# The first load of y as eight transfers of 16 partitions in place of one of 128

## The chip, the cores and the metric

The kernel runs on one core of one Trainium2 chip. The metric is the device time of one execution in microseconds (us), lower being better. The median of three runs of the kernel before is 119.94 us (119.94 to 120.14).

## The reference

```python
B, S, D = 1024, 16, 512
x, y:  bfloat16 (B, S, D)        gamma: bfloat16 (D)

def reference(x, y, gamma):
    return x + gamma * y
```

Every row of 512 numbers of y is multiplied by the same gamma and added to the row of x. Read and written are x, y and the output, of 16.78 MB each: 50.33 MB in all.

## The kernel before

The 16,384 rows of x, y and the output are dealt out to the 128 partitions of SBUF: partition p holds rows 128 p to 128 p + 127, which lie one after the other in DRAM (L52 to L54). "Rows" from here on are the 128 rows of one partition, of 1,024 bytes each. The whole of y stays in SBUF (`y_sb`, 128 rows in each partition) and is worked on in place: it is multiplied by gamma, then x is added into it, then it is stored. x has a buffer of 64 rows only (`x_sb`), which is loaded twice.

The work is written down as lists, without a scheduler:

- `SP` (L10) is what the SyncE queue issues, in this order: y rows 0 to 64, x rows 0 to 64, y rows 64 to 128, x rows 64 to 117, x rows 117 to 128. The last two go into places of `x_sb` that earlier rows held, so SP waits for the adds that free them (`frees`, L85; the wait is at L107).
- `ACT` (L11) is what the ScalarE queue issues: the row of gamma, then the stores of rows 0 to 64 and 64 to 128. The first store waits also until x rows 64 to 117 have landed (`RELEASE`, L16; TensorE passes the news on at L135 to L137).
- `DVE` (L18) is the order on VectorE: multiplies ('m') and adds ('a') of four pieces of 53, 11, 53 and 11 rows (`PIECES`, L6): m0, m1, a0, a1, m2, m3, a2, a3. Each is one instruction over 128 partitions (L156, L165). `need` (L141) puts the waits for the loads ahead of them: m0 waits for the y load that holds its rows, a0 for the x load.

The function `ring` (L96) walks through such a list and issues one DMA for each entry. One load of 64 rows is a DMA of 128 partitions, each with 64 rows that lie one after the other in DRAM and in SBUF, 65,536 bytes. Every load has a semaphore of its own, which a finished DMA raises by 16; `_take` (L22) waits for a count and takes it off again. VectorE waits for 16 before the first use of a load (L147).

`EARLY` (L13) says how many entries of each list are issued before everything else. The last lines (L173 to L179) take these DMA instructions out of their place and put them at the head of the program, ahead of the barrier at which the engines meet at its beginning (it appears in the waits as L41). It is (1, 0): the first load of y is issued there, before SP goes to the barrier; the other loads and gamma are issued after it.

gamma is spread over the partitions with a matmul of a row of ones with the row of gamma (L130), which VectorE copies to SBUF as bfloat16 (L132). The first multiply needs it.

Of the kernel before, what the change touches and what calls it, by code (L numbers as in the profile page):

```python
# [15 lines left out]
RELEASE = ('x', 64, 117, 0)  # L16

DVE = [('m', 0), ('m', 1), ('a', 0), ('a', 1), ('m', 2), ('m', 3), ('a', 2), ('a', 3)]  # L18
MULT, ADD = mybir.AluOpType.mult, mybir.AluOpType.add


def _take(sem, n, eng):  # L22


    return eng.wait_ge(sem, n).then_inc(sem, -n)  # L25


def kernel(
# [9 lines left out]
    nc = tc.nc  # L38
    P = nc.NUM_PARTITIONS
# [13 lines left out]
    yv = yf.rearrange("(p n) d -> p n d", p=P)  # L53
# [5 lines left out]
    y_sb = nc.alloc_sbuf_tensor("y_sb", [P, rows, D], dt).ap()  # L59
    x_loads = [w for w in SP + ACT if w[0] == "x"]  # L60
    y_loads = [w for w in SP + ACT if w[0] == "y"]
# [9 lines left out]
    s_load = {w: sem("s_" + "_".join(map(str, w[:2]))) for w in x_loads + y_loads}  # L71
    s_add, s_go, s_rel, s_end, s_out = sem("s_add"), sem("s_go"), sem("s_rel"), sem("s_end"), sem("s_out")
    added = [a for kind, *a in DVE if kind == "a"]
    order = {a[0]: k for k, a in enumerate(added)}

    def meets(a, b, c, d):
        return a < d and c < b

    def pieces_of(a, b):
        return [c for c in range(n) if meets(starts[c], starts[c + 1], a, b)]  # L80
# [4 lines left out]
    def frees(w):  # L85

        c = set()
        for v in x_loads[: x_loads.index(w)]:
            lo, hi = max(v[3], w[3]), min(v[3] + v[2] - v[1], w[3] + w[2] - w[1])
            if lo < hi:  # L90
                c |= set(pieces_of(v[1] + lo - v[3], v[1] + hi - v[3]))
        return sorted(c)

    early = []

    def ring(eng, what, n_early):  # L96

        known, went = 0, False
        for k, w in enumerate(what):
            kind = w[0]  # L100
            need = frees(w) if kind == "x" else pieces_of(w[1], w[2]) + list(w[3:]) if kind == "s" else []
            need = max((order[c] + 1 for c in need), default=0)
            if kind == "s" and not went:
                _take(s_go, 1, eng)
                went = True
            if need > known:
                eng.wait_ge(s_add, need)  # L107
                known = need
            if kind == "g":
                i = eng.dma_start(out=gamma_row, in_=gamma.unsqueeze(0)).then_inc(s_gamma, 16)  # L110
            elif kind == "x":
                to = x_sb[:, w[3] : w[3] + w[2] - w[1], :]
                i = eng.dma_start(out=to, in_=xv[:, w[1] : w[2], :]).then_inc(s_load[w], 16)
            elif kind == "y":
                r = slice(w[1], w[2])
                i = eng.dma_start(out=y_sb[:, r, :], in_=yv[:, r, :]).then_inc(s_load[w], 16)
            else:
                r = slice(w[1], w[2])
                i = eng.dma_start(out=ov[:, r, :], in_=y_sb[:, r, :]).then_inc(s_out, 16)
            if k < n_early:  # L120
                early.append(i.ins)

    ring(nc.sync, SP, EARLY[0])
    ring(nc.scalar, ACT, EARLY[1])


# [14 lines left out]
    def need(loads, c):  # L141
        for w in loads:
            if w not in landed and meets(starts[c], starts[c + 1], w[1], w[2]):
                if w == RELEASE:
                    _take(s_rel, 1, nc.vector)
                else:
                    _take(s_load[w], 16, nc.vector)  # L147
                landed.add(w)

    for kind, *args in DVE:  # L150
        c = args[0]
        yt = y_sb[:, starts[c] : starts[c + 1], :]
        if kind == "m":
            need(y_loads, c)
            g = gamma_sb[:, None, :].to_broadcast([P, PIECES[c], D])
            nc.vector.tensor_tensor(out=yt, in0=yt, in1=g, op=MULT).then_inc(s_dve, 1)  # L156
            open_mults += 1
        else:
            need(x_loads, c)
            if open_mults:  # L160
                _take(s_dve, open_mults, nc.vector)
                open_mults = 0
            at = x_at(starts[c])
            xt = x_sb[:, at : at + PIECES[c], :]
            nc.vector.tensor_tensor(out=yt, in0=xt, in1=yt, op=ADD).then_inc(s_add, 1)  # L165
# [44 lines left out]
```

## Time and profile before

| what | before |
|---|---|
| median of 3 runs | 119.94 us |
| the profiled execution | 119.93 us |
| its span, first to last instruction | 118.6 us |
| multiply or add of 53 rows (L156, L165) | 14.3 us each, two of either |
| multiply or add of 11 rows | 3.1 us each, two of either |
| first multiply starts | 21.94 us |
| first add starts | 41.39 us |
| reloads of x issued on SP | from 55.71 us |
| stores issued on ACT | from 76.88 us |
| HBM read and written | 33.56 and 16.78 MB |

The span starts with the first instruction, which is SP's issue of the first load of y. An engine's busy time counts its instructions; a DMA instruction only issues, and its packets then run on the core's 16 DMA engines, of which the page shows the busy share and the bytes moved in slices of time. A packet is counted in the slice in which it starts, with its whole length, so that shares above 1 occur in short slices. Queue q1 is SP's, q10 is ACT's. The small packets of a few bytes are those that raise the semaphores.

### The profile page before, as it was taken

Reading aid. Unit: us, or ns where it says so; the run is one execution under the profiler, and the core shown is the slowest. Engines: PE = TensorE matmul, PEld = TensorE weight load, DVE = VectorE, ACT = ScalarE, POOL = GpSimd, SP = SyncE. Lnnn points to the kernel's source line nnn. Section 1 sums busy time; section 2 is a strip of 40 time slices with the busy share of each in tenths; the row PEclk is TensorE's granted clock in tenths of the full one; section 3 lists DMA queues with packets and bytes.
Section 4 is the critical chain, followed back from the end, with each engine's and each line's share of the span. In section 5 each row is a group of like instructions: output and inputs, shape, how many; then the busy total and the mean of one; then the engine's idle time right before and its main releaser. Section 6 shows DMA issues by size and latency. Waiting matters only on the chain. (4 is left out here: it accounts for less than half of the span.)

```text
span 118.6 us, 78 instructions
## 1 busy us (share of the span) xinstructions
PE 0.6 (0%) x1; PEld 0.1 (0%) x1; DVE 70.0 (59%) x10; POOL 0.2 (0%) x4
## 2 busy tenths in 40 slices
PE   0001000000000000000000000000000000000000
PEld 0000000000000000000000000000000000000000
DVE  0002000599999299999759999999999910000000
POOL 0000000000000000000000000000000000000000
DMA  9889888998899888998896969598899888988892
GB/s 354 354 376 685 354 354 354 597 464 354 354 398 663 354 354 354 663 398 354 354 586 293 586 293 567 220 639 354 354 575 486 354 354 376 685 354 354 354 619 88
DMA packets 1010, 50.33 MB, mean 424 GB/s; under 512 B 113, under 2 KB 114, under 8 KB 114
## 3 DMA queue, kind: packets, MB, share of 16 engines
q1 hardware_dynamic: 720, 33.55, 66.0%
q10 hardware_dynamic: 290, 16.78, 32.6%
HBM read 33.56 MB, written 16.78 MB: 424 GB/s over the span
## 5 line engine op out<-in xcount | busy, mean ns | idle before, releaser
L156 DVE TENSOR_TENSOR y_sb<-y_sb,gamma_sb 128x27136 bf16<-128x27136 bf16 (+1 forms) x4 | 34.6, 8688 | 12.7 <-DVEq L25 12.7
L165 DVE TENSOR_TENSOR y_sb<-x_sb,y_sb 128x27136 bf16<-128x27136 bf16 (+1 forms) x4 | 34.6, 8688 | 2.3 <-DVEq L25 2.2
L132 DVE CAST gamma_sb<-gamma_ps 128x512 bf16<-128x512 f32 x1 | 0.7, 692 | 8.8 <-DVEq L25 8.8
L127 DVE MEMSET ones_row<- 1x128 bf16 x1 | 0.2, 165 | 1.5 <-PEq L41 1.5
L130 PE MATMUL gamma_ps<-gamma_row,ones_row 1*128 1x512 bf16 x1 | 0.6, 578 | 9.7 <-PEq L25 9.7
L130 PEld LDWEIGHTS gamma_ps<-gamma_row,ones_row 1*128 1x128 bf16 x1 | 0.1, 100 | 9.7 <-issue 9.7
L194 POOL MEMSET const-uint8-127<- 128x1 uint8 x1 | 0.1, 102 | 0.0
L194 POOL MEMSET const-bfloat16-1.0<- 128x1 bf16 x1 | 0.1, 101 | 0.0
L194 POOL MEMSET const-float32-0.0<- 128x1 f32 x1 | 0.1, 98 | 0.2 <-issue 0.2
L194 POOL MEMSET const-float32-1.0<- 128x1 f32 x1 | 0.1, 98 | 0.0
## 6 DMA issues: line engine op xcount, KB each, us to landing
x_sb<-in_x_dram SPq DMA_DIRECT2D x1, 6784.0 KB, 20.8
x_sb<-in_x_dram SPq DMA_DIRECT2D x1, 1408.0 KB, 23.9
y_sb<-in_y_dram SPq DMA_DIRECT2D x2, 40.2
out_dram<-y_sb ACTq DMA_DIRECT2D x2, 22.8
x_sb<-in_x_dram SPq DMA_DIRECT2D x1, 39.7
gamma_row<-in_gamma_dram ACTq DMA_DIRECT2D x1, 1.0 KB
```

What stands on the lines that cost most here:

```text
L127: nc.vector.memset(ones_row, 1.0).then_inc(s_ones, 1)
L130: nc.tensor.matmul(gamma_ps, ones_row, gamma_row, start=True, stop=True).then_inc(s_ps, 1)
L132: nc.vector.tensor_copy(out=gamma_sb, in_=gamma_ps).then_inc(s_dve, 1)
L156: nc.vector.tensor_tensor(out=yt, in0=yt, in1=g, op=MULT).then_inc(s_dve, 1)
L165: nc.vector.tensor_tensor(out=yt, in0=xt, in1=yt, op=ADD).then_inc(s_add, 1)
L194: nc = _bacc.Bacc("TRN2", target_bir_lowering=False, num_devices=1)
```

## The change

The first entry of the list with y, rows 0 to 64, is issued as eight DMAs. DMA number j takes the partitions j, j + 8, j + 16 and so on to j + 120, 16 in all, with the same 65,536 bytes for each partition; together they move the same bytes to the same places. All eight are put at the head of the program, ahead of the barrier. They raise one semaphore, and VectorE waits for 16 x 8 = 128 before the first multiply. The other loads, the stores and the arithmetic stay.

```diff
+GROUP = 8
...
             elif kind == "y":
                 r = slice(w[1], w[2])
-                i = eng.dma_start(out=y_sb[:, r, :], in_=yv[:, r, :]).then_inc(s_load[w], 16)
+
+                step = GROUP if w == y_loads[0] else 1
+                for j in range(step):
+                    to, of_ = y_sb[j:P:step, r, :], yv[j:P:step, r, :]
+                    i = eng.dma_start(out=to, in_=of_).then_inc(s_load[w], 16)
+                    if step > 1:
+                        early.append(i.ins)
...
-            if k < n_early:
+            if k < n_early and i.ins not in early and w != y_loads[0]:
                 early.append(i.ins)
...
-                    _take(s_load[w], 16, nc.vector)
+                    _take(s_load[w], 16 * GROUP if w == y_loads[0] else 16, nc.vector)
```

## The prediction

> **What bounds the kernel now.** I read the table of busy time first, then the line of the DMA engines in the 40 slices, the queues, and then short windows of the span, since the table names no bound by itself.
>
> ```profile
> span 118.6 us, 78 instructions
> PE 0.6 (0%) x1; PEld 0.1 (0%) x1; DVE 70.0 (59%) x10; POOL 0.2 (0%) x4
> ...
> DMA  9889888998899888998896969598899888988892
> ...
> DMA packets 1010, 50.33 MB, mean 424 GB/s; under 512 B 113, under 2 KB 114, under 8 KB 114
> ...
> q1 hardware_dynamic: 720, 33.55, 66.0%
> q10 hardware_dynamic: 290, 16.78, 32.6%
> ```
>
> VectorE is busy for 59% of the span, but the packets of the two queues fill 66.0 + 32.6 = 98.6% of 16 engines' time. There is no slice in which they rest. The kernel is bound by its 16 DMA engines from the first packet to the last, so a cost to the packets goes straight to the end. The chain of waits does not show this (it holds two adds and "issue"), since no instruction stands for the transfer that ends last.
>
> The length of one packet comes from windows of 1 us (columns: busy time and count of each engine, clock, share of the 16 DMA engines, GB/s; a packet is booked whole in the window in which it starts):
>
> ```profile
> 1.00:2.00 1.00, 0.00 (x0) 0.00 (x0) 0.17 (x1) 0.00 (x0) 1.00 2.92 983
> 11.00:12.00 1.00, 0.00 (x0) 0.00 (x0) 0.15 (x1) 0.00 (x0) 1.00 2.42 1049
> ```
>
> In 11 to 12 us, 1049 GB/s over 1 us is 1.049 MB, that is 16 packets of 65,536 bytes, one for each engine; a share of 2.42 says that each took 2.42 us. So an engine moves 65,536 / 2.42 = 27.1 GB/s, 16 of them 433. The 50.33 MB are 48 such packets for each engine: 48 x 2.42 = 116.2 us. What remains of the 118.6 us lies at the two ends. In 1 to 2 us, 983 GB/s is 15 packets, with a share of 2.92: 2.92 x 16 / 15 = 3.11 us each, 0.7 us more than later ones. The same view with 0.1 us windows shows when these packets start, and when the last round does:
>
> ```profile
> 0.90:1.00 0.10, 0.00 (x0) 0.00 (x0) 0.00 (x0) 0.00 (x0) 1.00 1.90 655
> 1.00:1.10 0.10, 0.00 (x0) 0.00 (x0) 0.00 (x0) 0.00 (x0) 1.00 10.09 3277
> ...
> 1.60:1.70 0.10, 0.00 (x0) 0.00 (x0) 0.08 (x1) 0.00 (x0) 1.00 1.69 655
> ```
>
> ```profile
> 4.00:4.10 0.10, 0.00 (x0) 0.00 (x0) 0.00 (x0) 0.00 (x0) 1.00 1.51 655
> ...
> 4.50:4.60 0.10, 0.00 (x0) 0.00 (x0) 0.00 (x0) 0.00 (x0) 1.00 4.54 1966
> ...
> 115.20:115.30 0.10, 0.00 (x0) 0.00 (x0) 0.00 (x0) 0.00 (x0) 1.00 1.51 655
> ...
> 115.80:115.90 0.10, 0.00 (x0) 0.00 (x0) 0.00 (x0) 0.00 (x0) 1.00 1.51 655
> ```
>
> 655 GB/s in 0.1 us is one packet. The first packets start between 0.9 and 1.7 us, the second ones between 4.0 and 4.6, the last whole ones between 115.2 and 115.9: the engine that is late at 4.6 us is late by as much at the end. Start (1.0 to 1.6) + 0.7 + 116.2 gives 117.9 to 118.5, and the last semaphore and wait end the span.
>
> [...] of packets under 512 B there are 113, which is 16 for each of seven transfers of 128 partitions and 1 for gamma's single row. [...]
>
> **The change, part by part.**
> Spreading. Transfer j touches partitions j, j+8, ..., j+120. [...] eight packets per engine. [...] a packet takes 2 x 2.42 = 4.84 us: 8 x 4.84 = 38.7 us in place of 8 x 2.42 = 19.4. That adds 19.4 us. [...] I take 19.4[...].
>
> Does anything hide it? No: the DMA engines have no slack (98.6%), and the rest follows them. The first multiply starts at 21.94 us, after 10.8 us of idle time that the landing of y ends; the first add at 41.39 us waits for x, behind y on the same rings. VectorE, the reloads of x and the stores all move back together; the idle 2.2 us before that add stay. After y the old spreading is back, at the old rate.
>
> Issuing. The trace's DMA instructions on SP take 0.37, 0.33 and 0.45 us. Eight for one are 7 x 0.37 = 2.6 us more before SP reaches the starting barrier. All engines wait there, so gamma and the first x load, issued at 1.43 us, go out near 4.0; the second y load, at 1.81, near 4.4. Cover: x must be in the rings by about 21 us, 17 us later. Gamma's chain ends with the cast at 10.46 + 0.69 = 11.15 us and would end near 13.8, 8 us ahead of the old 21.94 (and far ahead of a later one). The eight follow each other at about 0.4 us, each with 2.42 us of work, so no engine runs dry. Cost 0; only an issue of over 2.4 us would uncover it.
>
> Semaphores. 7 x 16 more small packets, 7 on each engine. At the old end of y (window 20 to 22 us: share 1.21, as in any stretch that catches one start of every engine) no gap shows. Between 0 and 0.1 us in all; I take 0.05. The wait counts to 128 in place of 16 on the same instruction, which holds up nothing else.
>
> Start. A short transfer may give all 16 engines their first descriptor sooner. If the first starts, spread over 0.6 us, fell together with the earliest, the late engines would win about 0.5 us; if the spread comes from serving 16 engines one after another, 0. I take 0.15.
>
> Sum: 19.4 + 0 + 0.05 - 0.15 = 19.3. The profiled execution took 119.93 us for a span of 118.6; the median of the runs is 119.94, so the sum is put on that: 139.2 us. The likeliest case's own range is 129.6 to 142.
>
> **Rivals.**
> A. [...] (119.6 us, the other side). [...] packets stay at 2.42 us and only the start counts: a gain of up to 0.5 us less 0.05, I take 0.3, so 119.64. [...]
> B. The same without the gain (119.9): the spread of the starts comes from the engines being served in turn. For it: a DMA instruction costs 0.52 us even for gamma's one row, so the rows do not set its length.
> C. [...] (121.4). [...] the other eight would start with the fifth issue, 4 x 0.37 = 1.5 us late (at most 4 x 0.45 = 1.8). Every engine still has 48 packets, so the end moves by the 1.5 us: 121.4. [...]
>
> **How the numbers follow.** Ports 0.66, C 0.08, B 0.11, A 0.15. No change means within 0.2%, 0.24 us, about what a measurement of this kernel can tell. A is faster, B the same; ports and C slower: 0.15, 0.11, 0.74. The range leaves out A and the tail above 142 and takes in the others: 119.7 to 142.
>
> **What would show it.** Right: from 1 to 40 us the DMA engines busy at about 217 GB/s, packets of 4.84 us; the first multiply near 41 us; from then on 2.42 us packets and every later event 19 us back; under 512 B 225 packets. If the first multiply starts before 22.2 us and packets take 2.42 us, [...] (A or B: the starts tell which). Half of the first packets starting 1.5 us late would be C. [...]

## The result, and the profile after

| | before | changed |
|---|---|---|
| median of 4 runs each | 120.0 us | 141.51 us (141.44 to 141.59) |
| profiled execution, and its span | 119.93, 118.6 us | 141.47, 140.1 us |
| first multiply starts | 21.94 us | 43.63 us |

The ratio is 1.179 (95% interval 1.177 to 1.181): the change costs 21.5 us, where the forecast had 19.3. The page of the changed kernel, its first line, the DMA engines in 40 slices, the packets and the queues:

```profile
span 140.1 us, 85 instructions
...
DMA  9929909939949697998969699798969696989976
GB/s 299 243 56 299 300 0 299 299 75 224 299 150 449 299 580 318 486 412 374 524 299 599 299 496 480 325 434 376 582 299 599 299 599 299 524 374 449 449 337 262
DMA packets 1123, 50.33 MB, mean 359 GB/s; under 512 B 226, under 2 KB 227, under 8 KB 227
...
q1 hardware_dynamic: 832, 33.56, 70.8%
q10 hardware_dynamic: 290, 16.78, 27.6%
```

The engines are still busy for 70.8 + 27.6 = 98.4% of the time, and the bytes are the same, but the mean rate fell from 424 to 359 GB/s. So the engines do not wait for work; a part of the packets takes longer. Q1's small packets rose by 112, that is by 16 for each of the seven additional transfers (one more packet of a few bytes is another queue's, q14). The twos and zeros of the DMA line are no rest: a packet is booked where it starts, and long packets leave slices without a start.

Which packets, is seen in windows of about one round each, in which 16 packets start, one for each engine (233 GB/s over 4.5 us are 1.049 MB; columns as in the prediction: window and its length, busy time and count of PE, PEld, DVE and POOL, clock, DMA share, GB/s):

```profile
1.30:5.80 4.50, 0.00 (x0) 0.00 (x0) 0.00 (x0) 0.00 (x0) 1.00 1.05 233
...
16.10:21.20 5.10, 0.58 (x1) 0.10 (x1) 0.69 (x1) 0.00 (x0) 1.00 1.00 206
21.20:26.10 4.90, 0.00 (x0) 0.00 (x0) 0.00 (x0) 0.00 (x0) 1.00 1.01 214
...
31.20:36.30 5.10, 0.00 (x0) 0.00 (x0) 0.00 (x0) 0.00 (x0) 1.00 1.01 206
...
41.40:44.60 3.20, 0.00 (x0) 0.00 (x0) 0.97 (x1) 0.00 (x0) 1.00 0.91 328
44.60:47.00 2.40, 0.00 (x0) 0.00 (x0) 2.40 (x1) 0.00 (x0) 1.00 1.01 437
```

Window length times share is the mean length of a packet: 4.7 us in the first round, 5.1 in the others, 4.9 in the fifth, then 2.9 in the round that follows y and 2.4 again from 44.6 us on. The records of the packets themselves say 4.72, 5.11, 4.94, 2.89 and 2.42. The slow packets are exactly the 128 of the first y load, eight rounds of 16. The fifth round is a little shorter than the others, and so it is in the kernels e3, e9 and e10 below (4.96, 4.93 and 4.85 us); why is not shown.

The start of the timeline (start and length in us, engine, line, operation, count, and idle time before):

```profile
0.00 5.01 SPq L122 DMA_DIRECT2D y_sb<-in_y_dram  x8
...
6.31 0.34 SPq L115 DMA_DIRECT2D x_sb<-in_x_dram  x1
6.32 0.53 ACTq L112 DMA_DIRECT2D gamma_row<-in_gamma_dram  x1
...
17.88 0.58 PE L138 MATMUL gamma_ps<-gamma_row,ones_row 1*128 1x512 bf16 x1 [17.88 <-PEq L27]
18.61 0.69 DVE L140 CAST gamma_sb<-gamma_ps 128x512 bf16<-128x512 f32 x1 [12.04 <-DVEq L27]
43.63 17.30 DVE L164 TENSOR_TENSOR y_sb<-y_sb,gamma_sb 128x27136 bf16<-128x27136 bf16 x2 [24.33 <-DVEq L27]
62.97 17.29 DVE L173 TENSOR_TENSOR y_sb<-x_sb,y_sb 128x27136 bf16<-128x27136 bf16 x2 [2.04 <-DVEq L27]
...
98.46 18.85 ACTq L127 DMA_DIRECT2D out_dram<-y_sb  x2
```

SP issues for 5.01 us ahead of the barrier, in place of 0.37; x and gamma go out 4.9 us later, and gamma is ready at 19.3 us. The multiply, at 43.63, waits 24.33 us for y alone. The rest of the kernel follows at its old distances: the first add and the stores are both 21.58 us later than before (41.39 and 76.88 us then).

### The profile page after: what moved, and what is told of

Same layout as the page of the kernel before. It is cut to its first block, busy times and chain, and to the rows that moved or that the text cites. A ratio compares the mean times of both kernels' runs of the same rounds, so it can differ in the third digit from the quotient of the medians.

```text
span 140.1 us, 85 instructions
## 1 busy us (share of the span) xinstructions
PE 0.6 (0%) x1; PEld 0.1 (0%) x1; DVE 70.0 (50%) x10; POOL 0.2 (0%) x4
## 3 DMA queue, kind: packets, MB, share of 16 engines
q1 hardware_dynamic: 832, 33.56, 70.8%
q10 hardware_dynamic: 290, 16.78, 27.6%
```

## The experiments

The suspect is the SBUF side: which partitions the engines write at the same time. "Port theory" in the expectations is the name for this assumption, that some sets of partitions make the engines hold each other up and others do not; the prediction's "ports" is the case with doubled packets. No record shows where on the way into SBUF this would happen; the runs show which sets of partitions are fast and which are slow. Its rivals: the eight issues and their semaphores; the place in DRAM, since the rows of one transfer now lie at a distance of 1 MB (8 partitions of 131,072 bytes); that each transfer has only one packet for each engine (the one-descriptor theory); the start of the program. All the edits are in the loop that issues the y load; e7 alone moves it to another load. The times of e1 and e11 are medians of 12 and 8 executions, the others are of one execution each; the kernel before took 119.87 to 120.46 us beside them, so that a difference of several us can be read from one.

**e1_row_split: eight transfers, all 128 partitions in each.**

```diff
-                    to, of_ = y_sb[j:P:step, r, :], yv[j:P:step, r, :]
+                    q = slice(w[1] + 8 * j, w[1] + 8 * j + 8)
+                    to, of_ = y_sb[:, q, :], yv[:, q, :]
```

> The first load of y is again issued as eight transfers ahead of the barrier, but each takes 8 of the 64 rows of all 128 partitions (8,192 bytes for a partition, eight descriptors for an engine). Port theory [...]: [...] the 21.5 us are gone and the time is within 0.5 us of 120.0; the first multiply starts near 22.3 us. Issue theory (eight issues, eight semaphores and a later barrier cost the time): it stays near 141. If only the start counts, the 0.4 us by which the first packet came later (1.37 in place of 1.00 us) would show how much of it is due to eight issues.

Measured: 120.2 us, ratio to before 1.0016 (1.0007 to 1.0025). From its timeline, and a window within the first y load:

```profile
0.00 4.06 SPq L123 DMA_DIRECT2D y_sb<-in_y_dram  x8
...
22.19 17.29 DVE L166 TENSOR_TENSOR y_sb<-y_sb,gamma_sb 128x27136 bf16<-128x27136 bf16 x2 [11.37 <-DVEq L27]
```

```profile
10.00:14.00 4.00, 0.00 (x0) 0.00 (x0) 0.69 (x1) 0.00 (x0) 1.00 1.01 428
```

The eight issues take 4.06 us on SP, gamma and x go out at 5.1, the first multiply starts at 22.19 us, and the rate within the load is close to the old one (428 against 433 GB/s). So eight issues ahead of the barrier with 112 more semaphore packets cost 0.2 us at most. The smaller packets alone can account for it: 309 ns for 8,192 bytes, where an eighth of 2.42 us is 302, so that the packets of this load sum to 20.37 us for each engine in place of 20.04. The issue theory falls.

**e2_next_16 and e4_sbuf_next_dram_8th, e3_sbuf_8th_dram_next: the SBUF side against the DRAM side.**

```diff
-                    to, of_ = y_sb[j:P:step, r, :], yv[j:P:step, r, :]
# e2
+                    to, of_ = y_sb[16 * j : 16 * j + 16, r, :], yv[16 * j : 16 * j + 16, r, :]
# e3
+                    to, of_ = y_sb[j:P:8, r, :], yv[16 * j : 16 * j + 16, r, :]
# e4
+                    to, of_ = y_sb[16 * j : 16 * j + 16, r, :], yv[j:P:8, r, :]
```

> Eight transfers of 16 partitions that lie next to each other (16 j to 16 j + 15) in place of every eighth. Port theory: [...] a packet takes 4 x 2.42 = 9.7 us or, with the surcharge of the changed kernel (5.11 in place of 4.84), 10.2; the load takes 77 to 82 us, the kernel 178 to 183 us. HBM theory (engines that read at a distance of 1 MB in DRAM collide): the distance is now 128 KB, the packets are back near 2.42 us and the time near 120. One-descriptor theory (a packet that is alone in its transfer, with a semaphore write after it, is slow whatever its place): 5.1 us a packet and 141.5 us as in the changed kernel.

> SBUF side as in the changed kernel (partitions j, j + 8, ...), DRAM side as with neighbours (blocks 16 j to 16 j + 15), so that the first 64 rows of y go to other partitions than their own and that half of the output is computed from other rows of y. Port theory: 5.1 us a packet, 141.5 us, since only the SBUF side counts. HBM theory: near 120. One-descriptor theory: 141.5.

> The crossed case: SBUF partitions 16 j to 16 j + 15, DRAM blocks j, j + 8, ..., so that the first 64 rows of y go to other partitions than their own and that half of the output is computed from other rows of y. Port theory: [...] 178 to 183 us, whatever the DRAM side does. HBM theory: as the changed kernel, 141.5. One-descriptor theory: 141.5.

Measured: 174.6 us (e2), 141.32 (e3), 175.64 (e4). Windows of about one round, first of e2, then of e3, then of e4:

```profile
17.90:27.10 9.20, 0.58 (x1) 0.10 (x1) 0.69 (x1) 0.00 (x0) 1.00 1.01 114
27.10:36.40 9.30, 0.00 (x0) 0.00 (x0) 0.00 (x0) 0.00 (x0) 1.00 1.00 113
```

```profile
31.30:36.40 5.10, 0.00 (x0) 0.00 (x0) 0.00 (x0) 0.00 (x0) 1.00 1.01 206
```

```profile
27.60:37.00 9.40, 0.00 (x0) 0.00 (x0) 0.00 (x0) 0.00 (x0) 1.00 1.00 112
```

The packet follows the SBUF side: 5.1 us with every eighth partition, 9.3 or 9.4 with 16 neighbours, whichever blocks of DRAM they are read from. Between e2 and e4, which differ in the DRAM side alone, lie 0.13 us a packet (9.27 and 9.40), between e3 and the changed kernel nothing (5.11 in both). The HBM theory falls, and so does the one-descriptor theory, since all four kernels have one packet for each engine in a transfer, and two of them take nearly twice as long for it as the other two. The 9.27 us are less than the 9.7 to 10.2 that were expected: the direction of the assumption is right, its arithmetic, with four times 2.42 us, only near. That factor of four was the author's estimate. By the packet records the engines start one round over 1.86 us in e2 and over 1.63 us in e4, so for that time packets of two transfers are in flight; whether this makes the packets shorter no run tests.

**e10_every_4th_of_64: which 16 partitions.**

```diff
-                    to, of_ = y_sb[j:P:step, r, :], yv[j:P:step, r, :]
+                    a = 64 * (j // 4) + j % 4
+                    to, of_ = y_sb[a : a + 61 : 4, r, :], yv[a : a + 61 : 4, r, :]
```

> Eight transfers of 16 partitions, every fourth of 64 (a, a + 4, ..., a + 60). [...] Port theory: 5.1 us a packet and about 141.4 us again. [...] as it does with 128 partitions, and the packets would be 2.42 us, about 120.4.

Measured: 140.84 us, 5.08 us a packet; the expectation's other figures, 2.42 us and 120.4, are out. One round of it:

```profile
30.70:35.80 5.10, 0.00 (x0) 0.00 (x0) 0.00 (x0) 0.00 (x0) 1.00 1.00 206
```

Every fourth of 64 partitions does as badly as every eighth of 128 (5.08 and 5.11 us), so it is not the step of eight that makes a packet slow.

**e7_second_load: not the start.** The first y load is one transfer again, and the same eight are made of the second, in their place in the list (the diff is against the kernel before):

```diff
-                i = eng.dma_start(out=y_sb[:, r, :], in_=yv[:, r, :]).then_inc(s_load[w], 16)
+                if w == y_loads[1]:
+                    for j in range(GROUP):
+                        to, of_ = y_sb[j:P:8, r, :], yv[j:P:8, r, :]
+                        i = eng.dma_start(out=to, in_=of_).then_inc(s_load[w], 16)
+                else:
+                    i = eng.dma_start(out=y_sb[:, r, :], in_=yv[:, r, :]).then_inc(s_load[w], 16)
...
-                    _take(s_load[w], 16, nc.vector)
+                    _take(s_load[w], 16 * GROUP if w == y_loads[1] else 16, nc.vector)
```

> The first load of y is one transfer again; instead the second (rows 64 to 128), which is issued at 1.8 us and runs from 40 us on, is issued as eight transfers of every eighth partition. Port theory: eight packets of 5.1 us in place of 2.42 on every engine, 8 x 2.69 = 21.5 us more, about 141.3 us, while the first multiply stays at 21.9 us and the second y load takes 41 us. Start theory (the loss belongs to the beginning of the program, where the queues are empty and SP is late): about 120.

Measured: 141.4 us. Its windows, the last round of the first x load and two of the second y load:

```profile
37.80:40.20 2.40, 0.00 (x0) 0.00 (x0) 1.45 (x1) 0.00 (x0) 1.00 1.01 437
49.80:54.90 5.10, 0.00 (x0) 0.00 (x0) 5.10 (x1) 0.00 (x0) 1.00 1.01 206
...
60.00:64.80 4.80, 0.00 (x0) 0.00 (x0) 0.00 (x0) 0.00 (x0) 1.00 1.02 218
```

The first multiply stays at 21.95 us. The slow packets (5.1 us in the window from 49.8 us) go along with the eight transfers, 40 us after the start, and cost about the same, 21.5 us (against 119.87 us of the kernel before beside it); the fifth round is the shorter one here too (4.9 us).

**e5_half_engines and e8_half_engines_odd_first: transfers of 8 partitions on half of the engines.** A miss that the second run narrows down.

```diff
-GROUP = 8
+GROUP = 16
...
-                    to, of_ = y_sb[j:P:step, r, :], yv[j:P:step, r, :]
# e5
+                    a = 32 * (j // 4) + j % 4
# e8
+                    a = (64, 96, 0, 32)[j // 4] + j % 4
# both
+                    to, of_ = y_sb[a : a + 29 : 4, r, :], yv[a : a + 29 : 4, r, :]
```

> The first load of y as sixteen transfers of 8 partitions (a, a + 4, ..., a + 28), each with one descriptor for each of 8 engines, [...] the other 8 engines have no part in this load. Port theory: [...] a packet takes 2.42 us; 8 engines then have 16 + 40 packets, 56 x 2.42 = 135.5 us in place of 116.2, and the time is 120.0 + 19.3 = 139.3, up to 140 with the later start: 1.5 to 2.2 us less than the changed kernel, though half of the engines are left out. One-descriptor theory: 5.1 us a packet on these engines, 16 x 2.7 us more again, near 182 us.

e5 took 160.94 us, neither figure. Its windows, when y is alone, two rounds with x beside it, and later:

```profile
2.00:12.00 10.00, 0.00 (x0) 0.00 (x0) 0.00 (x0) 0.00 (x0) 1.00 0.49 210
...
16.70:19.20 2.50, 0.58 (x1) 0.10 (x1) 0.45 (x1) 0.00 (x0) 1.00 0.98 420
19.20:21.70 2.50, 0.00 (x0) 0.00 (x0) 0.25 (x1) 0.00 (x0) 1.00 0.97 419
...
26.00:60.00 34.00, 0.00 (x0) 0.00 (x0) 0.00 (x0) 0.00 (x0) 1.00 1.02 214
```

From 2 to 12 us half of the engines work (share 0.49) and move 210 GB/s, as much as all 16 in the changed kernel: 210 GB/s over 10 us are 32 packets, of 0.49 x 16 x 10 / 32 = 2.45 us. One packet for each engine in a transfer is not slow by itself. With x beside it the share is 0.97 to 0.98 and the rate 419 to 420 GB/s, but from 26 to 60 us all 16 engines are busy (share 1.02) and together move only 214 GB/s. By the packet records the change comes with the ninth packet of y, which starts at 21.7 to 22.2 us: from there to 62 us a packet takes 4.3 to 5.1 us. The step that the expectation had overlooked: from its ninth transfer on, this load writes partitions 64 to 127. So y on partitions 0 to 63 runs beside x at full rate, and y on partitions 64 to 127 does not. That the packets of x were then going to partitions 64 to 127 as well, and that the two loads held each other up there, is the author's estimate; the records name no engine and no partition. If it is so, turning the order round must undo most of it:

> The sixteen transfers of 8 partitions of the run on half of the engines, with the order turned round: partitions 64 to 127 [...] first, then 0 to 63 [...]. Port theory: [...] so they can meet only from about 13 us (when x is issued) to about 21 us, three or four packets: 139.3 us for the uneven work plus about 9, so 145 to 151 us in place of 160.9. If eight engines with short transfers are slow for another reason, the order makes no difference: 161.

Measured: 147.45 us, in the range that was computed. The slow packets now lie where y writes partitions 64 to 127 with x beside it, three rounds between 14 and 29.5 us (184 GB/s from 19 to 24 us, 197 from 24 to 29). With the same transfers and bytes, the order of the two halves alone is worth 13.5 us. A window after that, 32 to 56 us, in which y writes partitions 0 to 63 (until the first multiply, at 49.41 us) with x beside it:

```profile
32.00:56.00 24.00, 0.00 (x0) 0.00 (x0) 6.59 (x1) 0.00 (x0) 1.00 0.97 418
```

**e6_four_of_32, e11_four_of_32_timed and e9_four_of_next_32: 32 partitions.**

```diff
-GROUP = 8
+GROUP = 4
...
# e9, in place of every fourth
+                    to, of_ = y_sb[32 * j : 32 * j + 32, r, :], yv[32 * j : 32 * j + 32, r, :]
```

> The first load of y as four transfers of 32 partitions (every fourth), two descriptors for an engine. [...] Port theory, partitions dealt to the engines in order (2 e and 2 e + 1 to engine e, or e and e + 16): [...] 5.1 us a packet, about 141. Port theory, dealt by the same rule as 128 partitions[...]: 2.42 us a packet, about 120. One-descriptor theory: the packets that stand ahead of another packet of the same transfer are fast, about 130.

> Four transfers of 32 neighbouring partitions (32 j to 32 j + 31) in place of every fourth. It tells how 32 partitions are dealt to the engines. [...] 9.3 us a packet as with 16 neighbours, 8 packets, about 174 us. In order (2 e and 2 e + 1 to engine e): [...] 5.1 us, about 141. By the partition's own number: [...] 2.42 us a packet and 120 to 125 us.

Measured: e6 120.39 us with 2.42 us a packet, e9 141.11 with 5.11. One window of each, e6 first:

```profile
9.10:11.50 2.40, 0.00 (x0) 0.00 (x0) 0.00 (x0) 0.00 (x0) 1.00 1.01 437
```

```profile
30.70:35.80 5.10, 0.00 (x0) 0.00 (x0) 0.00 (x0) 0.00 (x0) 1.00 1.01 206
```

Both have four transfers of 32 partitions and the same bytes; every fourth partition moves at the full rate, 32 neighbours at less than half of it. How the 32 are dealt to the engines stays open: the 5.11 us of e9 are what its expectation has for dealing in order, but e6, with 2.42 us, does not have the 5.1 us that its own names for that. The measured times thus tell which sets of partitions are slow, not which engine serves which partition.

> The four transfers of every fourth partition once more, timed. [...] what is left is the start. In the single look the first packets came at 1.32 us where one transfer of 128 partitions has them at 1.00, and the instruction took 0.55 us in place of 0.37. If a partition step in the SBUF pattern costs this start and nothing after it takes it back, the kernel is 0.3 to 0.5 us slower than before, a ratio of 1.003 to 1.004; if the start is hidden by the shorter transfers, 1.000.

Measured: 120.37 us, ratio 1.003 (1.0019 to 1.004). This is the cost of the start alone, with packets at the full rate. Of the kernels whose first load is on 16 engines, those with a partition step on the SBUF side take 0.55 to 0.58 us for their first instruction and have the first packets after 1.3 us: the changed kernel, e3, e6, e10. Those without it have 0.37 to 0.38 us and 1.00: before, e1, e2, e4, e9. A step on the DRAM side alone (e4) makes no difference, nor does the number of partitions from 16 to 128. On eight engines (e5, e8, with a step) it is 0.78 us and 1.51. One window of e3 and the same of e4, before e3's first packet:

```profile
0.90:1.20 0.30, 0.00 (x0) 0.00 (x0) 0.00 (x0) 0.00 (x0) 1.00 0.00 0
```

```profile
0.90:1.20 0.30, 0.00 (x0) 0.00 (x0) 0.00 (x0) 0.00 (x0) 1.00 17.35 2185
```

The series in one table, on all 16 engines:

| partitions of a transfer | us for 65,536 bytes | all 16 engines |
|---|---|---|
| all 128 (before) | 2.42 | 433 GB/s |
| every fourth, 32 (e6) | 2.42 | 433 GB/s |
| every eighth, 16 (changed kernel, e3, e7) | 5.11 | 205 GB/s |
| every fourth of 64, 16 (e10) | 5.08 | 206 GB/s |
| 32 neighbours (e9) | 5.11 | 205 GB/s |
| 16 neighbours (e2, e4) | 9.27, 9.40 | 113, 112 GB/s |

The last column is 16 x 65,536 bytes over the time. The number of partitions alone does not set the time: 32 take 2.42 or 5.11 us, 16 take 5.08 to 9.40.

## Why the prediction was right

- Spreading, the main step: shown. The slow packets are those of the first y load and follow the partitions that its SBUF side writes (5.11 us in the changed kernel and e3, 9.27 and 9.40 in e2 and e4); in e1 and e6 the same load in several transfers does not cost the 20 us (120.2 and 120.39 us). What holds the engines up is not shown.
- Its size: 2.42 us more on each of eight packets had been taken, a plain doubling, which was the author's estimate. It is a little more: 5.11 us in place of 4.84. The first round grew by 4.72 - 3.11 = 1.6 us, six rounds by 2.69, the fifth by 4.94 - 2.42 = 2.5: 20.25 us in place of 19.4. Another 0.5 us were not in the sum at all: the first round of x took 2.89 us in place of 2.42. The first of these packets took 3.16 us, the last 2.57; that the first ones still ran beside packets of y is a likely reason, not tested alone.
- Nothing hides it: right. The first multiply moved by 21.69 us, the end by 21.5.
- Issuing: free as said, but mis-sized. Eight issues took 5.01 us, not 3.0, because one with a partition step takes 0.57 to 0.61 us; x and gamma went out 4.9 us later, not 2.6. The cover held, and e1 shows it: 4.06 us of issues for a loss of 0.2. But that of gamma was thinner than named: its chain ended at 19.30 us, not near 13.8, which is 2.6 us ahead of the old multiply and not 8.
- Start: the wrong sign. A gain of 0.15 us was taken; the first packets came at 1.37 in place of 1.00 us, spread over 1.0 us in place of 0.6, on the mean of the 16 engines 0.54 us later. e11 prices the start of four such transfers at 0.3 us.
- Together: on the mean of the engines the last packet ended 21.4 us later. By the packet records this is 0.54 us of start, 20.25 in the packets of y, 0.04 in the gaps between them, where the semaphore packets run (0.05 was taken), 0.47 in the first round of x, and 0.08 in all that follows.
- The range: its upper end of 142 was the author's estimate. That 141.5 lies within it, 0.5 us from the top, is in part luck; that packets more than doubled (2.42 to 5.11 us), and where, is not.
- Rivals A and B are out, since no packet of this load kept its 2.42 us. C is out: half of the engines would have begun with the fifth issue, at 2.52 us, but all 16 first packets had started by 2.4 us.

## What to carry to other kernels

Where the DMA engines bound a kernel, look at which partitions each transfer writes, not only at the engines that it uses: with every eighth partition 16 busy engines moved 206 GB/s in place of 433, with 16 neighbours 112 to 114, while the DMA engines stayed busy (shares of 1.00 to 1.01). If a load must be split, split its rows and keep the 128 partitions (0.2 us for eight pieces), or take every fourth of all 128 partitions (0.3 us for four). With two loads in flight at once, the order in which one of them writes its partitions counts too (160.94 and 147.45 us in e5 and e8).

## What the runs showed that was not expected

- With every eighth partition a packet takes more than twice its time, 5.11 us in place of 2 x 2.42 = 4.84. Why is not shown, nor what sets the 27.1 GB/s of one engine at the full rate.
- A partition step in the SBUF pattern makes the DMA instruction 0.2 us longer (0.57 against 0.37) and its first packet 0.3 to 0.4 us later; on 16 engines the number of partitions and a step in DRAM do neither.
- 32 partitions, every fourth, move at the full rate, 2.42 us a packet; all 128 are not needed for that.
